# Two attention blocks on one core: load order of the start, one pool for two PSUM banks, and some exponentials on VectorE

## The chip, the cores and the metric

The kernel runs on one core of one Trainium2 chip. The metric is the time of one execution on the device in microseconds (us), lower is better. Times are medians of a few executions. A profile belongs to one execution. I compare each kernel with runs of the kernel before that were taken on the same chip in the same rounds. Executions of one kernel spread by 0.1% to 0.7% here (up to 8 us), so I do not read differences of 2 or 3 us between kernels.

## The reference

Two blocks of 32 heads with head size 32, sequence 2048, model size 1024, everything in bf16; the outputs are concatenated.

```python
# block A: plain multi-head attention over 2048 keys
q, k, v = split_heads(x @ wqkv)                    # 32 heads of 32
p = softmax(q @ k.T * 32 ** -0.5)                  # 2048 x 2048 for every head
a = merge_heads(p @ v) @ wo
# block B: four segments of 512; causal softmax inside a segment,
# plus a linear memory of the earlier segments, mixed by a gate g
for s in range(4):
    a_dot = softmax(q_s @ k_s.T * scale + mask) @ v_s
    a_mem = (phi(q_s) @ M) / (phi(q_s) @ z + 1e-6)
    o_s   = g * a_mem + (1 - g) * a_dot
    M, z  = M + phi(k_s).T @ v_s, z + sum(phi(k_s))
b = merge_heads(o) @ wo
out = concat([a, b], axis=-1)
```

Block A exponentiates 32 x 2048 x 2048 scores, block B some more. That is what the kernel's time goes into.

## The kernel before

The kernel does not write its instructions in a fixed order. While it is being built, it runs a small scheduler: processes ask for engine time, PSUM banks and buffers, and a model of the engines (durations, priorities, pools) decides which instruction comes next on each engine. The result is a fixed order per engine, with semaphores. Any edit, also one of a priority, reorders thousands of instructions. And a process that waits for a bank or buffer from a pool makes the order itself wait.

The kernel uses eight banks of PSUM. Three pairs take scores, one bank (OB) takes the output of the P times V matmuls ("PV"), one bank (SB) takes everything else ("side jobs": projections, memory, output projections).

```python
PAIRS = [(0, 1), (2, 3), (4, 5)]
OB, SB = 6, 7
RING = 20                          # half pairs of exponentiated scores kept in SBUF: 10 pairs

def s_batch(self, u, k):           # one batch of scores: two pairs, 8 matmuls of 256 columns
    ...
    prs = yield acq(self.pairs, npair)            # 2 of the 3 pairs
    ...
    yield do("PE", lambda e: f(e, mms), r=keys, w=w, cost=N256, prio=0, mode=ROW)
    for x in range(npair):
        Q.spawn(self.exps(u, k, x, prs[x], slots[x], one))

def exps(self, u, k, x, pr, sl, one):             # one pair: 128 x 1024 scores
    ...
    yield do("ACT", lambda e: e.activation(ap, self.ps[:, pr[0]:pr[1] + 1, :], ACTF.Exp, scale=SCALE), ...)
    Q.give(self.pairs, [pr])
    ...

def pv_unit(self, u, steps, half):
    ...
    yield acq(self.obank, 1)       # the one output bank; finish() gives it back
    ...

# start (cut): weights first, x behind them, transposing loads of the rest of x at once
for k in (0, 1, 2):
    Q.spawn(self.load_WA(k, 0, 0, "SP" if k == 0 else "ACT"))
Q.spawn(self.rest_x())
```

A batch of scores needs two of three pairs. While ScalarE works on the second pair of a batch, one pair is free, and the other pair that the next batch needs is the one whose exponential (the first of the batch) has just ended. So the scores of the next batch start when the exponential of the first pair has ended, and run while ScalarE works on the second pair.

## Time and profile before

1183.4 us, median of three runs (1181.3 to 1183.8); the profiled one took 1181.5 us on the core. First the page: span, busy times, granted TensorE clock in tenths per fortieth of the span, the chain that ended last, and the costliest group.

```profile
span 1181.5 us, 49521 instructions
...
PE 1061.9 (90%) x23146; PEld 508.2 (43%) x23146; DVE 484.6 (41%) x1070; ACT 1120.2 (95%) x1223; POOL 125.9 (11%) x285
...
PEclk7999998999799999999999999899999999899999
...
ACT 66%; PE 25%; DVE 5%; DMA 2%; issue 1%; POOL 0%; ACTq 0%; SPq 0%; DVEq 0%
...
L861 ACT ACTIVATE PT<-ps 128x1024 bf16<-128x1024 f32 x1168 | 1083.2, 1098 | 24.3 <-PE ps L844 23.6
```

ScalarE (ACT) is the limit and TensorE (PE) is close behind it. The 1168 exponentials of the last line, with 16 more that write other buffers, are nearly the whole of ACT. One record lasts 1098 ns, but that is not what one exponential costs: records overlap. In the trace, neighbouring exponentials start 904 ns apart (median), and I use this distance as the cost. The third row below is what remains of the span, so the ledger sums to it:

| part of the span | before, us |
|---|---|
| until the first exponential starts | 24.2 |
| ScalarE work: 1184 x 0.904 + 32 activations of the memory part | 1094.0 |
| exponentials that start later than that distance ("late") | 45.7 |
| from the end of the last exponential to the end | 17.6 |

The start, in the timeline (start and duration in us; a bracket tells how long the engine was idle and what ended that):

```profile
2.07 1.93 ACTq L549 DMA_DIRECT2D OTA<-in_A_x_dram  x2
...
13.02 2.74 PE L536 MATMUL ps<-ident,OTA 128*128 128x128 bf16 x24 [6.46 <-DMA OTA<-in_A_x_dram]
...
16.91 6.07 PE L591 MATMUL ps<-xA,WA 128*32 128x512 bf16 x64 [1.15 <-issue]
...
24.23 7.44 ACT L861 ACTIVATE WoB<-ps 128x1024 bf16<-128x1024 f32 x8 [7.42 <-PE ps L844]
```

TensorE waits until 13 us for three of the four x tiles, which are queued behind the weights. Then the first 64 projection matmuls take 6.07 us, because the clock is at half from 8.2 to 21.9 us (first digit of the clock row).

### The profile page before, as it was taken

To read this page: it belongs to the slowest core of one execution; us is meant where nothing else is said; L and a number is where in the kernel's file an instruction comes from. 1 tells how busy PE (TensorE), PEld (TensorE's weight loads), DVE (VectorE), ACT (ScalarE), POOL (GpSimd) and SP (SyncE) were. 2 spreads that over 40 slices of the span, in tenths; PEclk is the share of its full clock that TensorE was granted. 3 is DMA by queue.
4 is the path that set the end of the run, shared out by engine and by line. 5 is a ranking of instruction groups with operands and counts; after the bars stand their busy time and mean duration, and the time that the engine had idled before them with its cause. 6 is when DMAs were issued, how large, how long until landed. Compare 5 with 4: busy or idle time off the path is not lost.

```text
span 1181.5 us, 49521 instructions
## 1 busy us (share of the span) xinstructions
PE 1061.9 (90%) x23146; PEld 508.2 (43%) x23146; DVE 484.6 (41%) x1070; ACT 1120.2 (95%) x1223; POOL 125.9 (11%) x285
## 2 busy tenths in 40 slices
PE   6889998988799898999899999889999999899997
PEld 2444443443344444444444444434444444344443
DVE  1224333333343545445434544445355543444232
ACT  2999999999899999999999999999999899999994
POOL 1002002001111111102101201111111110110000
PEclk7999998999799999999999999899999999899999
DMA  9532333224021223251222123131222122101111
GB/s 169 98 59 43 67 95 72 44 56 87 20 60 29 62 45 56 50 89 42 59 48 60 34 56 65 34 69 47 48 55 56 43 47 91 38 25 34 38 39 45
DMA packets 214837, 67.23 MB, mean 57 GB/s; under 512 B 203872, under 2 KB 212064, under 8 KB 214624
## 3 DMA queue, kind: packets, MB, share of 16 engines
q1 hardware_dynamic: 212256, 62.94, 24.8%
q8 instruction: 183, 3.00, 1.1%
q10 hardware_dynamic: 2368, 1.05, 0.4%
q14 instruction: 30, 0.25, 0.1%
HBM read 36.70 MB, written 8.39 MB: 38 GB/s over the span
## 4 chain that ended last, share of the span: by engine, by line
ACT 66%; PE 25%; DVE 5%; DMA 2%; issue 1%; POOL 0%; ACTq 0%; SPq 0%; DVEq 0%
ACT PT L861 64%; PE ps L591 8%; PE ps L937 7%; PE ps L844 4%; PE ps L1003 4%; ACT E L696 2%; DMA OTA<-in_A_x_dram 1%; DVE VT L597 1%; DMA VB<-VT 1%; DMA VA<-VT 1%; ACT WoB L861 1%; DVE Dt L959 1%; DVE md L722 1%; DVE Rb L962 1%; DVE QA L597 0%
## 5 line engine op out<-in xcount | busy, mean ns | idle before, releaser
L861 ACT ACTIVATE PT<-ps 128x1024 bf16<-128x1024 f32 x1168 | 1083.2, 1098 | 24.3 <-PE ps L844 23.6
L937 PE MATMUL ps<-PT,ones 128*32 128x256 bf16 (+1 forms) x4800 | 302.6, 274 | 0.0
L937 PE MATMUL ps<-PT,VA 128*32 128x256 bf16 x4032 | 258.9, 278 | 13.4 <-ACT PT L861 7.4
L844 PE MATMUL ps<-QA,KA 32*128 32x256 bf16 x4096 | 206.6, 276 | 33.1 <-ACT PT L861 26.5
L591 PE MATMUL ps<-xA,WA 128*32 128x512 bf16 x3072 | 218.2, 389 | 10.3 <-DVE md L722 2.2
L591 PE MATMUL ps<-xB,WB 128*32 128x512 bf16 x3072 | 213.8, 381 | 14.5 <-DVE QA L597 3.7
L870 POOL TENSOR_SCALAR_AFFINE_SELECT PT<-PT 128x256 bf16<-128x256 bf16 (+1 forms) x224 | 98.5, 440 | 900.2 <-ACT PT L861 893.9
L937 PEld LDWEIGHTS ps<-PT,VA 128*32 128x32 bf16 x4032 | 107.7, 96 | 104.7 <-issue 42.3
L844 PEld LDWEIGHTS ps<-QA,KA 32*128 32x128 bf16 x4096 | 61.1, 92 | 205.7 <-ACT PT L861 182.9
L937 PEld LDWEIGHTS ps<-PT,ones 128*32 128x32 bf16 x4800 | 130.3, 98 | 21.7 <-issue 0.5
L591 PEld LDWEIGHTS ps<-xA,WA 128*32 128x32 bf16 x3072 | 73.0, 97 | 83.7 <-issue 27.0
L591 PEld LDWEIGHTS ps<-xB,WB 128*32 128x32 bf16 x3072 | 74.3, 96 | 79.5 <-issue 45.4
L959 DVE STREAM_TRANSPOSE Dt<-ps 128x256 f32<-128x256 f32 x128 | 57.2, 447 | 124.2 <-PE ps L937 123.3
L597 DVE CAST KQB<-ps 128x512 bf16<-128x512 f32 x64 | 44.0, 688 | 147.5 <-PE ps L591 147.5
L1009 DVE CAST outsb<-ps 128x512 bf16<-128x512 f32 x61 | 42.0, 689 | 118.8 <-PE ps L1003 118.8
L597 DVE CAST VT<-ps 128x512 bf16<-128x512 f32 x64 | 43.8, 684 | 95.0 <-PE ps L591 92.2
L1003 PE MATMUL ps<-WoB,OTB 128*32 128x512 bf16 x1024 | 71.4, 381 | 2.0 <-DVE outsb L1009 0.7
L1003 PE MATMUL ps<-xA,OTA 128*32 128x512 bf16 x1024 | 67.2, 384 | 1.0 <-DVE outsb L1009 0.7
L937 PE MATMUL ps<-PT,VB 128*32 128x256 bf16 (+1 forms) x768 | 47.6, 269 | 13.5 <-DVE tB L984 3.8
L962 DVE STREAM_TRANSPOSE Rb<-Rall 128x256 f32<-128x256 f32 x128 | 56.6, 442 | 3.6
L597 DVE CAST KA<-ps 128x512 bf16<-128x512 f32 x32 | 22.0, 689 | 67.3 <-PE ps L591 67.3
L844 PE MATMUL ps<-KQB 32*128 32x128 bf16 (+3 forms) x512 | 43.7, 304 | 3.8 <-ACT PT L861 2.2
(70 smaller groups left out, 466.5 us busy)
## 6 DMA issues: line engine op xcount, KB each, us to landing
WB<-in_B_wk_dram SPq DMA_DIRECT2D x32, 256.0 KB, 2.9
WB<-in_B_wq_dram SPq DMA_DIRECT2D x32, 256.0 KB, 2.9
WB<-in_B_wv_dram SPq DMA_DIRECT2D x32, 256.0 KB, 3.2
out_dram<-outsb SPq DMA_DIRECT2D x64, 128.0 KB, 1.8
WA<-in_A_wqkv_dram SPq DMA_DIRECT2D x22, 256.0 KB, 2.9
WoB<-in_B_wo_dram SPq DMA_DIRECT2D x1, 2048.0 KB, 9.7
xA<-in_A_wo_dram SPq DMA_DIRECT2D x1, 2048.0 KB, 8.5
WA<-in_A_wqkv_dram ACTq DMA_DIRECT2D x2, 256.0 KB, 5.8
```

Of the source, the lines that this page charges most:

```text
L591: ins = e.matmul(self.ps[32 * c:32 * c + 32, bank, :], W[:, i, 32 * c:32 * c + 32], x(i), start=(i == 0), stop=(i == NI - 1))
L597: return e.tensor_copy(dst, self.ps[:, bank, :])
L696: yield do("ACT", lambda e: e.activation(self.E[:, k0:k1, :], KQ[:, k0:k1, :], ACTF.Exp), r=kq, w=["E"], cost=0.093 + 0.427 * nk, prio=-1)
L722: yield do("DVE", lambda e: e.transpose(self.md[:, :], self.ps[:, bank, :]), r=[("ps", bank)], w=["md"], cost=dve(512), prio=1)
L844: ins = e.matmul(self.ps[:, bk, col:col + w], lhs(t, hs), rhs(q0, w, hs), start=True, stop=True)
L861: yield do("ACT", lambda e: e.activation(ap, self.ps[:, pr[0]:pr[1] + 1, :], ACTF.Exp, scale=SCALE), r=[("ps", bk) for bk in pr], w=keys, ...
L870: yield do("POOL", lambda e, m=m, n=n: e.affine_select(m, m, pattern=[[0, n], [1, P]], compare_op=ALU.is_ge, fill=0.0, base=0, channel_mul ...
L937: ins = e.matmul(out, l, r, start=st, stop=sp)
L959: yield do("DVE", lambda e: e.transpose(Dt[:, :], den), r=[("ps", OB)], w=[("Dt", x)], cost=dve(QU), prio=0)
L962: yield do("DVE", lambda e: e.transpose(Rb[:, :].rearrange("p (a b) -> p a b", b=32), self.spread(Rc)), r=[("Rc", ui)], w=[("Rb", x)], cos ...
L1003: ins = e.matmul(self.ps[32 * c:32 * c + 32, bank, :], lhs(j)[:, 32 * c:32 * c + 32], W(j), start=(j == 0), stop=(j == NG - 1))
L1009: return f(self.outsb[ob][:, :], self.ps[:, bank, :])
```

## The change

Its intent: let ScalarE start earlier, take a little work off it, and keep the score matmuls on time. The diff has some 260 changed lines; cut to its core:

```diff
 # start: x first, then the weights; the transposing loads wait until x has landed
-        for k in (0, 1, 2):
-            Q.spawn(self.load_WA(k, 0, 0, "SP" if k == 0 else "ACT"))
+        def first_w():
+            yield ("ev", ("XS", 2)); yield ("ev", ("XS", 3))
+            Q.spawn(self.load_WA(0, 0, 0, "SP")); Q.spawn(self.load_WA(1, 0, 0, "ACT"))
+            ...
 # start: warm-up matmuls behind each of the four groups of transposes
+            yield self.warm((4, 4, 4, 8)[t])
 # output bank and side bank in one pool, PV first
-            yield acq(self.obank, 1)
+        OB, = yield acq(self.side, 1, -1000)
 # 43 times: one bank of the second pair of a batch is exponentiated on VectorE
+        if (u, k, x) in self.off:                  # x is always 1
+            Q.spawn(self.exps_dve(pr[1], ...))     # six VectorE operations
+            yield do("ACT", lambda e: e.activation(..., self.ps[:, pr[0], :], ACTF.Exp, scale=sc), ...)
 # exps_dve: 2^t from bits. The exponent is kept as it is, the fraction goes through a cubic
+        z = max(scores, -122 * 2**23) + BIAS       # to int32, reads PSUM
+        u = (z & 0x7fffff) | 0x3f800000            # fraction, as a float in 1..2
+        z = z & 0x7f800000                         # power of two
+        p = (((u + C2) * u + C1) * u + C0) * z     # three scalar_tensor_tensor
 # memory for it: ring 20 -> 26 half pairs, one output buffer of block B instead of two
-RING = 20
+RING = 26
-        self.OTB = [sb(f"OTB{i}", [P, NG, 512]) for i in range(2)]
+        self.OTB = sb("OTB", [P, NG, 512])
 # the scheduler's model: margins for waits, a longer tail of PE; its parameters chosen anew
-    par = dict(b=(18, 14, 10), mem=-2, memM=2, span=66, rate=0.58, ahead=20, sl=4, ...)
+    par = dict(b=(14, 10, 3), mem=-4, memM=2, span=50, rate=0.6, ahead=20, sl=5, ..., mg=0.05, off=0.75, ...)
```

Also: the queries of block A are scaled in their projection so that `exps_dve` can read the exponent from the bits of a score, block B's operation T is merged into the next one, output buffers go from six to four, projections hold their place on TensorE once begun, PV goes first at the end, and the last drain of the output overlaps the reading of a flag.

## The prediction

> **What bounds the kernel now.** ScalarE. The page gives ACT 1120 us of a 1181.5 us span (95%), and the chain of waits is 66% ACT, nearly all of it the 1184 exps of a 128x1024 bank pair. In the timeline neighbouring exps start 904 ns apart (median), so they take 1184 x 0.904 = 1070 us; the 32 exps of E add 24 us. The first exp starts at 24.2 us, the last ends at 1163.6 us: 1139 us for 1094 us of work, so 45 us go to late starts (the view of waits names 31 us: score matmuls not there). The rest is a 24 us start and an 18 us tail. PE is 90% busy, DVE 41%.
>
> **What the change does, costed.**
> 1. Start. Weights are queued first now, and the last x tiles land only at about 13 us; the clock is at half from 8.2 to 21.9 us, so the 64 first projection matmuls take 6.1 us. With x first, transposing loads held back and warm-up matmuls in between, I expect x at 7 us, projection from 10 us, mostly at full clock (3.5 us), first exp at 15 us: 9 us saved, all on the path.
> 2. VectorE exps. 0.75 x 58 units = 43 half pairs go to DVE. ACT work falls by 512 elements each, 904 to an estimated 477 ns, 18 us in all. Not all arrives: a batch needs two of three pairs, so its scores start only after the exp of the previous batch's first half ends (its start + 1.05 us), plus the median 0.18 us until PE starts, 0.40 us of score matmuls, 0.05 us. That loop of 1.6 to 1.7 us fits in 2 x 0.904 but not in 0.904 + 0.477. I count 0.15 to 0.2 us each: 7 us. DVE pays six operations, about 3.7 us each time, 160 us in all: DVE goes to some 55%.
> 3. One pool for output and side banks, a ring of 13 instead of 10 pairs, margins in the order, PE's latency modelled longer. The next output can start while the last is normalised, but side jobs then lack a bank. I give it 13 of the 45 us of late exps. No engine work is saved, except the T operation (11 us of DVE, off the path).
> 4. Tail. PV goes first once scores are done (now 30 groups of projection matmuls come first, 6.6 us), and the output drain overlaps the flag read: 4 us.
>
> Sum: 1183 - 9 - 7 - 13 - 4 = 1150; I say 1149 us, 80% in 1132 to 1165. Chances: faster 0.80, same 0.18, slower 0.02.
>
> **What would show it.** First exp at 13 to 18 us. 43 ACT activations of 128x512 from PSUM, ACT busy near 1100. Behind each of them a gap on ACT of 0.15 to 0.35 us, waiting for scores; if those gaps are missing, step 2 is worth 18 us. DVE busy 610 to 660 us. Late exps below 35 us apart from those gaps. Last exp to end 13 to 15 us.
>
> **What would make it wrong.** PE becomes the limit: its work is unchanged while the span shrinks, so it would be 93% busy, and the window 900 to 950 us (PE 48 of 50 us, ACT 46.4) is already bound by it. Half-clock episodes (41 us after the start) fall differently with every order. Longer DVE queues delay evacuations and so side banks. If the new order removes most late exps, the time is below 1135.
>
> The Trainium skill ("ScalarE: Activation LUTs", Rules for kernel authors) has ScalarE as the only option for exp; the change bypasses that with bit operations and a cubic.

## The result, and the profile after

1155.0 us, median of four runs (1154.4 to 1159.7), against 1183.6 us for the kernel before in the same rounds (1181.3 to 1187.1). The ratio is 0.9765, 95% interval 0.9729 to 0.98. The same lines of the page:

```profile
span 1153.8 us, 49786 instructions
...
PE 1050.9 (91%) x23164; PEld 507.3 (44%) x23165; DVE 626.9 (54%) x1302; ACT 1103.9 (96%) x1223; POOL 127.4 (11%) x285
...
PEclk9999999999999999999999999999999999989999
...
ACT 55%; PE 32%; DVE 7%; DMA 4%; issue 1%; SPq 0%; POOL 0%; DVEq 0%
...
L891 ACT ACTIVATE PT<-ps 128x1024 bf16<-128x1024 f32 x1125 | 1045.3, 1101 | 21.3 <-PE ps L864 19.2
```

ScalarE is busy for 16 us less, VectorE for 142 us more, and TensorE and VectorE stand on the chain more often. The start, in the timeline:

```profile
9.11 0.61 PE L552 MATMUL ps<-ident,OTA 128*128 128x128 bf16 x8
...
11.38 3.64 PE L612 MATMUL ps<-xA,WA 128*32 128x512 bf16 x64
...
16.27 7.44 ACT L891 ACTIVATE WoB<-ps 128x1024 bf16<-128x1024 f32 x8 [5.49 <-PE ps L864]
```

The projections start 5.5 us earlier and run at full clock, 3.64 us instead of 6.07. The ledger, for the one profiled execution of each kernel:

| part of the span, us | before | after | difference |
|---|---|---|---|
| first exponential starts | 24.2 | 16.3 | -8.0 |
| ScalarE work | 1094.0 | 1075.6 | -18.4 |
| late, directly behind a half exponential | 0 | 15.4 | +15.4 |
| late, all others | 45.7 | 30.6 | -15.1 |
| tail | 17.6 | 15.8 | -1.8 |
| span | 1181.5 | 1153.8 | -27.7 |

(Differences are of the unrounded values.) The second and third row belong together. The 43 half exponentials take 43 x (0.904 - 0.477) = 18.4 us off ScalarE, and ScalarE then stands still for 15.4 us right behind them. One of them, in the timeline of the kernel after (lines of other work are left out):

```profile
107.33 2.08 ACT L891 ACTIVATE PT<-ps 128x1024 bf16<-128x1024 f32 x2
...
108.10 0.69 DVE L916 TENSOR_SCALAR ze<-ps 128x512 int32<-128x512 f32 x1 [0.73 <-PE ps L864]
...
109.14 0.77 ACT L885 ACTIVATE PT<-ps 128x512 bf16<-128x512 f32 x1
...
109.50 0.12 PEld L864 LDWEIGHTS ps<-QA,KA 32*128 32x128 bf16 x8 [0.42 <-ACT PT L891]
109.50 0.40 PE L864 MATMUL ps<-QA,KA 32*128 32x256 bf16 x8
...
109.95 2.85 ACT L891 ACTIVATE PT<-ps 128x1024 bf16<-128x1024 f32 x3
```

The two exponentials of the first line end at 109.41; the second of them is the first pair of the batch. The scores of the next batch follow at 109.50, 0.09 us later, and the exponential of these scores at 109.95. The half one (L885) started at 109.14 and could have let the next go at 109.62, so 0.33 us are lost. VectorE was not what held this up: its read of the other half (L916) was over by 108.79, and in all 43 cases it was over before the exponential ahead of the half one ended. In the 43 cases the scores start 0.056 us (median; up to 0.5 us where TensorE was busy with other work) after the exponential before the half one ended, and the next exponential starts 0.449 us (median) after the scores did; 0.346 us (median) of the 0.427 us saved are lost.

What the 43 pieces cost on VectorE, grouped by line (count, then busy time in us and mean ns of one):

```profile
L924 DVE SCALAR_TENSOR_TENSOR PT<-we,ze 128x512 bf16<-128x512 f32 x43 | 29.5, 686 | 0.8
L922 DVE SCALAR_TENSOR_TENSOR we<-ue 128x512 f32<-128x512 f32 x43 | 29.5, 686 | 0.0
L923 DVE SCALAR_TENSOR_TENSOR we<-we,ue 128x512 f32<-128x512 f32 x43 | 29.4, 685 | 0.6
L916 DVE TENSOR_SCALAR ze<-ps 128x512 int32<-128x512 f32 x43 | 28.9, 672 | 16.7 <-PE ps L864 16.7
L921 DVE TENSOR_SCALAR ze<-ze 128x512 int32<-128x512 int32 x43 | 18.1, 420 | 0.6
L919 DVE TENSOR_SCALAR ue<-ze 128x512 int32<-128x512 int32 x43 | 18.0, 417 | 0.3
```

These sum to 153 us, 3.57 us for each half bank that saves ScalarE 0.43 us. The two masks are the cheap ones, at 420 ns against 686 for the three `scalar_tensor_tensor`. That resembles what the Trainium skill states ("VectorE: DVE Perf Modes", the perf-mode tier table): it has fp32 `tensor_scalar` in SBUF in the 2x mode and fp32 `tensor_tensor` in the 1x mode; neither int32 nor `scalar_tensor_tensor` is in the table; here the int32 masks were the faster ones, like the former, and the `scalar_tensor_tensor` the slower ones, like the latter.

### The profile page after: what moved, and what is told of

Same layout as the page of the kernel before. It is cut to its first block, busy times and chain, and to the rows that moved or that the text cites. A ratio compares the mean times of both kernels' runs of the same rounds, so it can differ in the third digit from the quotient of the medians.

```text
span 1153.8 us, 49786 instructions
## 1 busy us (share of the span) xinstructions
PE 1050.9 (91%) x23164; PEld 507.3 (44%) x23165; DVE 626.9 (54%) x1302; ACT 1103.9 (96%) x1223; POOL 127.4 (11%) x285
## 4 chain that ended last, share of the span: by engine, by line
ACT 55%; PE 32%; DVE 7%; DMA 4%; issue 1%; SPq 0%; POOL 0%; DVEq 0%
ACT PT L891 52%; PE ps L612 12%; PE ps L994 9%; PE ps L864 6%; PE ps L1062 4%; DMA xB<-in_B_x_dram 2%; ACT E L718 1%; DVE Rb L1021 1%; DVE Dt L1018 1%; DMA VA<-VT 1%; DVE ze L916 1%; DVE VT L618 1%; DMA PKt<-PH 1%; ACT PT L885 1%; POOL PT L900 0%
## 5 line engine op out<-in xcount | busy, mean ns | idle before, releaser
L891 ACT ACTIVATE PT<-ps 128x1024 bf16<-128x1024 f32 x1125 | 1045.3, 1101 | 21.3 <-PE ps L864 19.2
L994 PE MATMUL ps<-PT,ones 128*32 128x256 bf16 (+1 forms) x4800 | 296.3, 274 | 0.0
L994 PE MATMUL ps<-PT,VA 128*32 128x256 bf16 x4032 | 252.6, 278 | 17.1 <-ACT PT L891 7.7
L864 PE MATMUL ps<-QA,KA 32*128 32x256 bf16 x4096 | 206.3, 276 | 47.7 <-ACT PT L891 42.6
L612 PE MATMUL ps<-xB,WB 128*32 128x512 bf16 x3072 | 208.1, 387 | 12.0 <-DMA xB<-in_B_x_dram 3.5
L612 PE MATMUL ps<-xA,WA 128*32 128x512 bf16 x3072 | 200.5, 381 | 2.1 <-DVE VT L618 0.5
L864 PEld LDWEIGHTS ps<-QA,KA 32*128 32x128 bf16 x4096 | 61.0, 92 | 214.6 <-ACT PT L891 192.8
L994 PEld LDWEIGHTS ps<-PT,VA 128*32 128x32 bf16 x4032 | 107.9, 97 | 84.1 <-issue 25.9
L994 PEld LDWEIGHTS ps<-PT,ones 128*32 128x32 bf16 x4800 | 129.9, 98 | 24.5 <-issue 0.3
L1018 DVE STREAM_TRANSPOSE Dt<-ps 128x256 f32<-128x256 f32 x128 | 56.4, 441 | 24.2 <-PE ps L994 23.3
L1062 PE MATMUL ps<-WoB,OTB 128*32 128x512 bf16 x1024 | 67.1, 381 | 0.5 <-DVE md L742 0.2
L1062 PE MATMUL ps<-xA,OTA 128*32 128x512 bf16 x1024 | 65.0, 381 | 0.3 <-DVE outsb L1068 0.2
L994 PE MATMUL ps<-PT,VB 128*32 128x256 bf16 (+1 forms) x768 | 46.2, 267 | 8.2 <-DVE OTA L1025 3.2
L864 PE MATMUL ps<-KQB 32*128 32x128 bf16 (+3 forms) x512 | 43.4, 302 | 3.9 <-ACT PT L891 2.9
L619 DVE TENSOR_SCALAR QA<-ps 128x512 bf16<-128x512 f32 x32 | 22.0, 688 | 41.0 <-PE ps L612 41.0
```

Source lines behind the costliest of these rows:

```text
L612: ins = e.matmul(self.ps[32 * c:32 * c + 32, bank, :], W[:, i, 32 * c:32 * c + 32], x(i), start=(i == 0), stop=(i == NI - 1))
L619: return e.tensor_scalar(dst, self.ps[:, bank, :], scale, None, ALU.mult)
L864: ins = e.matmul(self.ps[:, bk, col:col + w], lhs(t, hs), rhs(q0, w, hs), start=True, stop=True)
L994: ins = e.matmul(out, l, r, start=st, stop=sp)
L1018: yield do("DVE", lambda e: e.transpose(Dt[:, :], den), r=[("ps", OB)], w=[("Dt", x)], cost=dve(QU), prio=0, hold=0.15)
L1062: ins = e.matmul(self.ps[32 * c:32 * c + 32, bank, :], lhs(j)[:, 32 * c:32 * c + 32], W(j), start=(j == 0), stop=(j == NG - 1))
```

## The experiments

Theory after reading the result: the gain is 8 us of the start, 15 us of other late exponentials (which I had put down mainly to the shared pool), 2 us of tail, and almost nothing from VectorE's exponentials. Rivals: the halves help indirectly, through TensorE catching up in the gaps; the 15 us come from the ring, from the scheduler's margins, or from nothing but a fortunate order.

The kernel after serves as base unless I say otherwise. Twelve kernels ran, all gave correct results. "Late" is as in the ledger, "others" are the late ones not directly behind a half. Where I write "parameters chosen anew", I built several hundred settings of the scheduler's parameters for that variant and took the one whose planned order was shortest in the kernel's own planning; every time below is from the chip. All ratios are to the kernel before.

| kernel | median us | ratio [95%] | first exp | behind halves | others late | tail |
|---|---|---|---|---|---|---|
| after | 1155.0 | 0.9765 [0.9729, 0.9800] | 16.3 | 15.4 | 30.6 | 15.8 |
| no_dve_exps | 1155.5 | 0.9753 [0.9723, 0.9784] | 15.9 | 0 | 30.0 | 14.4 |
| no_dve_exps_tuned | 1159.8 | 0.9791 [0.9763, 0.9819] | 16.1 | 0 | 33.7 | 14.6 |
| half_first | 1167.4 | 0.9873 [0.9833, 0.9913] | 15.9 | 0.2 | 55.1 | 17.5 |
| old_start_loads | 1163.5 | 0.9819 [0.9788, 0.9850] | 24.5 | 15.5 | 32.0 | 15.6 |
| no_warm | 1156.0 | 0.9764 [0.9735, 0.9794] | 13.6 | 14.8 | 28.1 | 15.9 |
| own_obank | 1176.9 | 0.9935 [0.9895, 0.9974] | 16.9 | 14.7 | 52.6 | 15.3 |
| own_obank_tuned | 1157.8 | 0.9760 [0.9723, 0.9798] | 18.0 | 14.8 | 33.7 | 15.4 |
| ring20_tuned | 1162.2 | 0.9797 [0.9764, 0.9831] | 16.1 | 15.5 | 37.4 | 15.0 |
| neighbour | 1179.6 | 0.9945 [0.9910, 0.9980] | 15.9 | 13.6 | 55.9 | 17.6 |
| neighbour_b | 1170.6 | 0.9892 [0.9861, 0.9924] | 16.0 | 13.2 | 48.6 | 15.6 |
| hf_obank_tuned | 1147.7 | 0.9695 [0.9662, 0.9729] | 17.0 | 0.2 | 36.1 | 15.5 |
| hf_obank_b | 1146.0 | 0.9677 [0.9654, 0.9700] | 17.1 | 0.2 | 32.3 | 15.8 |

This table leaves out the granted clock, which differs between the kernels. In the profiled executions, between the first and the last exponential, some stretches run at half clock, and many of the other late exponentials start in these stretches or up to 1 us behind them (my count, good to a few us):

| kernel | half clock, us | others late there | others late elsewhere |
|---|---|---|---|
| before | 41 | 11 | 34 |
| after | 34 | 10 | 20 |
| no_dve_exps | 24 | 6 | 24 |
| own_obank | 72 | 27 | 26 |
| own_obank_tuned | 65 | 16 | 17 |
| hf_obank_tuned | 37 | 14 | 22 |
| hf_obank_b | 24 | 8 | 24 |

### No exponentials on VectorE: no_dve_exps and no_dve_exps_tuned

```diff
-    par = dict(..., off=0.75, ...)
+    par = dict(..., off=0.0, ...)
```

> The kernel after, with no half exp on VectorE (1184 full exps on ScalarE again), the rest unchanged. My theory: a half exp in the second pair of a batch gives back 0.35 of its 0.43 us, as the next scores wait for the exp of the first pair, so this part is worth 43 x 0.08 = 3 us and this kernel is at about 1158 us (1154 to 1162). Rival: the wait behind the halves lets PE catch up, so that part of the other late exps is spared too, and the part is worth its 18 us of ScalarE work: about 1173 us. A second rival is that VectorE's extra 160 us delay evacuations, so that this kernel is even faster than the kernel after.

Measured: 1155.5 us. The whole part is worth nothing that these runs can show; the first rival (18 us) falls clearly. In the ledger the 18.4 us of ScalarE work come back, the 15.4 us behind the halves go away, and the others stay, 30.0 against 30.6. So in sum no more than a few us of other waits were spared by the waits behind the halves or caused by VectorE's extra 153 us (second rival). A few us either way stay open: no_dve_exps was granted a little more clock (0.988 to 0.990 in its four executions, against 0.980 to 0.986), and away from half clock its others are 24 us against 20. My 3 us are within the spread.

> No half exps on VectorE, scheduling parameters chosen anew. If the exps on VectorE in the second pair are worth nothing, this is at or a little under 1155 us (1151 to 1156). If they are worth several us under a fitting order, then choosing anew does not help here and it stays at 1155 or above, as that order was already good.

Measured: 1159.8 us with parameters chosen anew for it, so choosing anew did not help. By the letter of what I had written, this leaves room for a gain of a few us from the VectorE exponentials. Since the same kernel with the old parameters took 1155.5 us, I take no more from it than that two orders of one kernel differ by 4 us, and that the better planned one was not the faster one.

### The half exponential in the first pair: half_first

If a half in the second pair is lost because the next scores wait for the first pair, then a half in the first pair should not be: it ends earlier, so the scores start earlier, and a full exponential hides them.

```diff
-                        self.off.add((u, k, 1))
+                        self.off.add((u, k, 0))
```

(and the same index where PV puts this batch later)

> The kernel after, with the 43 half exps moved from the second to the first pair of their batch. My theory: then the scores of the next batch wait for the half exp (done 0.43 us earlier) and a full exp of 0.90 us hides them, so the gap on ScalarE behind a half exp falls from a median of 0.35 us to under 0.1 us, and the time falls by 8 to 15 us, to about 1143 us. Rival: the pair is held by VectorE's first operation (0.69 us) or PE is the limit; then the gaps only move and the time stays within 4 us of 1155.

Measured: 1167.4 us, slower by 12 us, so the time missed my range altogether. But the gaps behind the halves did what the theory says; they are gone, 0.2 us for all 43. In the timeline:

```profile
107.32 0.69 DVE L916 TENSOR_SCALAR ze<-ps 128x512 int32<-128x512 f32 x1 [0.73 <-PE ps L864]
...
107.45 0.76 ACT L885 ACTIVATE PT<-ps 128x512 bf16<-128x512 f32 x1
107.93 5.78 ACT L891 ACTIVATE PT<-ps 128x1024 bf16<-128x1024 f32 x6
...
108.29 0.40 PE L864 MATMUL ps<-QA,KA 32*128 32x256 bf16 x8
```

The half starts at 107.45, the next full one 0.48 us later without a wait. The time was lost elsewhere: the others rose by 24.5 us, half of that in one place. ScalarE's own timeline, then TensorE's, around it:

```profile
590.68 1.94 ACT L891 ACTIVATE PT<-ps 128x1024 bf16<-128x1024 f32 x2 [0.20 <-PE ps L864]
605.29 1.94 ACT L891 ACTIVATE PT<-ps 128x1024 bf16<-128x1024 f32 x2 [12.67 <-PE ps L864]
```

```profile
592.57 0.23 PE L994 MATMUL ps<-PT,ones 128*32 128x128 bf16 x4
593.33 1.91 PE L1062 MATMUL ps<-WoB,OTB 128*32 128x512 bf16 x32 [0.53 <-DVE VT L618]
...
604.52 0.28 PE L994 MATMUL ps<-PT,VB 128*32 128x256 bf16 x4
...
604.84 0.40 PE L864 MATMUL ps<-QA,KA 32*128 32x256 bf16 x8
```

From 592.8 to 604.5 us TensorE runs only projections and memory matmuls: no PV (L994) and no scores (L864). It is not short of work, the scores are just not in the order there. PV and scores stop and resume together, while the output rows of a segment of block B are projected (L1062) from the buffer OTB, of which the change had left one out of two. By the code, an output of block B now takes one of two small buffers (tB) before its PV begins and keeps it until the memory part is ready and the previous segment's rows have been projected; without PV no place in the ring comes free, and without a place no scores are issued. I did not test this chain by a run of its own, so it is argued, not shown.

### Is it the order? Two controls: neighbour and neighbour_b

The last run raised a doubt about all of them: perhaps any edit costs some 10 or 20 us, as the parameters had been chosen for exactly the kernel after. So I moved one parameter by one step, and another one, without any change of engine work.

```diff
-    par = dict(..., sl=5, ...)
+    par = dict(..., sl=4, ...)          # neighbour
```
```diff
-    par = dict(..., span=50, ...)
+    par = dict(..., span=56, ...)       # neighbour_b
```

> A control: the kernel after with one scheduling parameter moved by one step (sl 5 to 4: from how few free ring pairs on the outputs get priority). No engine work changes. My theory now: the order of the kernel after is a lucky one of many, so that such a step alone costs 5 to 20 us (about 1165 us), as much as the parts that I undid singly. Rival: the order is robust, the time stays within 3 us of 1155, and the 21 us of the run with its own output bank is the value of the shared pool.

> A second control: the kernel after with the parameter span moved from 50 to 56 (how far ahead of use the projections are ordered). No engine work changes. If the order of the kernel after is one lucky order among many, this is slower too, by 5 to 25 us, most of it in one or two long waits for scores near 600 or 850 us. If only the other parameter (sl) was special, it is within 4 us of 1155.

Measured: 1179.6 us and 1170.6 us, that is 25 and 16 us slower than the kernel after, out of a gain of 29 us. The view of waits, ScalarE for score matmuls (sum in us, times, longest), of the kernels before and after, half_first, neighbour and neighbour_b, in this order:

```profile
ACT PT L861 <- PE ps L844: 23.6, 36, 1.6
```
```profile
ACT PT L891 <- PE ps L864: 19.2, 30, 1.6
```
```profile
ACT PT L891 <- PE ps L864: 32.6, 28, 12.7
```
```profile
ACT PT L891 <- PE ps L864: 40.1, 35, 9.8
```
```profile
ACT PT L891 <- PE ps L864: 34.9, 35, 9.8
```

The last number is what to look at. The bad orders hold single waits of 10 to 13 us; they end at 605 us (half_first), 857 us (neighbour) and 607 us (neighbour_b). In neighbour two more, of 6.7 us (before 613 us) and 4.0 us (before 69 us), make up 21 of its 25 us together with the first. (This view counts only idle time after a record's end, so its sums are smaller than the ledger's.) The kernel after has no long wait. A run that undoes a part and is slower therefore proves nothing about the part unless the parameters are chosen anew for it, and even then one order stands for each kernel.

### The shared pool: own_obank and own_obank_tuned

```diff
-        OB, = yield acq(self.side, 1, -1000)
+        OB, = yield acq(self.obank, 1)
-        self.side = Pool([SB, OB])
+        self.side = Pool([SB]); self.obank = Pool([OB])
```

(and the three places that give the bank back)

> The kernel after, with the output bank and the side bank fixed as in the kernel before, the rest unchanged. My theory: most of the 15 us of late exps that went away (other than behind half exps) came from the shared pool, so that late exps rise by 8 to 15 us and the time is about 1166 us. Rival: the gain came from the deeper ring and the margins of the order; then the time is within 4 us of 1155.

> The output bank fixed again as in own_obank, but with scheduling parameters chosen anew for it (ahead, b, mg, od, span). If the shared pool is worth something by itself, this stays at 1165 us or above; if the 21 us were only a bad order under parameters chosen for another kernel, it comes to 1150 to 1158 us, with late exps near those of the kernel after.

Measured: 1176.9 us with the parameters of the kernel after, as if the pool were worth 22 us, more than I had expected of it. Its longest wait for scores is 3.7 us; half of its late time falls into 72 us of half clock, so it is not bad in the way of the three above. With parameters chosen anew (ahead 22, b (16, 12, 6), mg 0.045, od 10, span 48) it took 1157.8 us, and its other late exponentials are 33.7 us against 30.6. So in these two orders the pool is worth some 3 us, which is within the spread, and own_obank_tuned had less clock on top (0.970 to 0.978 against 0.980 to 0.986). My theory, that most of the 15 us came from the pool, falls.

### The ring: ring20_tuned

```diff
-RING = 26
+RING = 20
```

(with parameters chosen anew; they put 36 halves on VectorE instead of 43)

> The kernel after with the ring of score buffers back at 10 pairs instead of 13, scheduling parameters chosen anew with it. If the deeper ring is what the late exps owe their fall to, late exps (other than behind half exps) are over 40 us and the time is 1163 us or more; if it is not, choosing anew brings it to 1153 to 1160 us, like the run with its own output bank.

Measured: 1162.2 us, other late exponentials 37.4 us. That lies between my two cases: 7 us more than in the kernel after, where orders of one kernel differ by as much. The deeper ring may be worth some us; the run does not settle it.

### The start: old_start_loads and no_warm

```diff
-        Q.spawn(first_w())                                   # old_start_loads
+        for k in (0, 1, 2):
+            Q.spawn(self.load_WA(k, 0, 0, "SP" if k == 0 else "ACT"))
-        yield ("ev", ("WA", 1, 0))                           # rest_x: when the transposing loads go
+        yield ("ev", ("XS", 3))
-                         r=[("XS", 3), ("XS", 2), ...] if c == 1 and t == 0 else [], w=...
+                         w=...
```
```diff
-            yield self.warm((4, 4, 4, 8)[t])                 # no_warm
+            pass
```

> The kernel after, with only the load order of the start put back: weights first, transposing loads not held back for the x tiles. Warm-up matmuls stay. My theory: the order of the loads is worth most of the 8 us by which the first exp starts earlier: first exp at 21 to 24 us, time about 1160 to 1163 us. Rival: the warm clock made the gain; then the first exp starts at 17 to 19 us and the time is under 1158 us.

> The kernel after without the warm-up matmuls between the transposes of the start (the first eight stay). I read the first exp, not the total. If the clock matters, the first 64 projection matmuls take about 6 us instead of 3.6 and the first exp starts at 17 to 19 us; if only the order of the loads matters, it starts at or before 16 us, and the matmuls were only in the way of the transposes.

Measured, old_start_loads: first exponential at 24.5 us, time 1163.5 us, other parts of the ledger as in the kernel after. The load order is the whole gain of the start; the run put back both sides of it together (weights first, transposing loads not held), so it does not part them. From its timeline:

```profile
17.38 0.61 PE L552 MATMUL ps<-ident,OTA 128*128 128x128 bf16 x8
...
19.65 3.64 PE L612 MATMUL ps<-xA,WA 128*32 128x512 bf16 x64
...
24.54 1.94 ACT L891 ACTIVATE WoB<-ps 128x1024 bf16<-128x1024 f32 x2 [5.50 <-PE ps L864]
```

With the late x tiles the warm-up matmuls did keep the clock for the projections (3.64 us), but they also stood in the way, so that the first exponential came no earlier than in the kernel before. From the timeline of no_warm:

```profile
4.64 2.92 PE L552 MATMUL ps<-ident,OTA 128*128 128x128 bf16 x32
...
8.71 3.64 PE L612 MATMUL ps<-xA,WA 128*32 128x512 bf16 x64 [1.15 <-ACT xA L561]
...
13.59 1.94 ACT L891 ACTIVATE WoB<-ps 128x1024 bf16<-128x1024 f32 x2 [4.98 <-PE ps L864]
```

Without the warm-up matmuls between the transposes the clock is full all the same (granted from 6.7 us on in this trace, from 5.5 us in the kernel after), and the first exponential starts at 13.6 us, 2.7 us earlier than in the kernel after. So in this profiled execution they only cost time. The total does not show it (1156.0 us; the profiled execution was the fastest, 1150.0, the others took up to 1157.6).

### Both together: hf_obank_tuned and hf_obank_b

half_first showed that the saved ScalarE time is real, and own_obank_tuned that the pool is not needed. So: halves in the first pair, output bank fixed, parameters chosen anew (two sets).

```diff
-                        self.off.add((u, k, 1))
+                        self.off.add((u, k, 0))
-        OB, = yield acq(self.side, 1, -1000)
+        OB, = yield acq(self.obank, 1)
-    par = dict(b=(14, 10, 3), ..., span=50, rate=0.6, ahead=20, ..., pv=18, ob=2, ..., od=8, ...)
+    par = dict(b=(15, 10, 4), ..., span=58, rate=0.585, ahead=22, ..., pv=19, ob=3, ..., od=2, ...)   # hf_obank_b
```

> Half exps in the first pair of their batch (the 43 us x 0.43 = 18 us of ScalarE work really saved), output bank fixed, scheduling parameters chosen anew. My theory: gaps behind half exps under 0.05 us, other late exps near 30 us, so about 1155 - 15 = 1140 us (1136 to 1146). Rival: PE is the limit (91% busy) and the saved ScalarE time comes back as other late exps, as in half_first (42 us apart from one 13 us wait); then about 1153 us.

> Half exps in the first pair and the output bank fixed, with a second set of scheduling parameters (near the first). If the 1148 us of the first set comes from the ScalarE work really saved, this is at 1144 to 1152 us as well; if it was a lucky order alone, it is at 1155 or above.

Measured: 1147.7 us, just outside my range of 1136 to 1146, and 1146.0 us with the second set (from a longer search), inside the range that I gave for that one. Both beat the kernel after (ratios 0.9695 and 0.9677 against 0.9765). The gaps behind halves are 0.2 us, the others 36.1 and 32.3. The nearest comparison is own_obank_tuned, which has the same bank layout, halves in the second pair, and parameters from a search as long as that of hf_obank_tuned: 1157.8 us. By the medians, 10 to 12 us of the 14.6 us that the gaps behind its halves cost arrived in the time (8 to 10 by the ratios).

This comparison has a flaw: own_obank_tuned was granted less clock (0.970 to 0.978, against 0.978 to 0.989 for the two), and its executions take longer with less of it (1159.7 us at 0.970, 1152.6 at 0.978). At the same 0.978 hf_obank_tuned took 1149.2 and 1151.0 us, so part of the 10 to 12 us may be the clock. The kernels without halves do not have this flaw: no_dve_exps and no_dve_exps_tuned had 0.983 to 0.990, no less on the whole than the two, and took 1155.5 and 1159.8 us. Against them the halves in the first pair gain 8 to 14 us of the 18.4, though the bank layout differs as well. That the gaps are gone is shown; how much of them arrives in the time is known only this roughly.

The view of waits of hf_obank_b, ScalarE for score matmuls:

```profile
ACT PT L891 <- PE ps L864: 12.4, 20, 1.3
```

There is no long wait in it. I did not run it without the warm-up matmuls of the start.

## Why the prediction was right or wrong

The measured 1155.0 us lies in the predicted range, 6 us above the 1149 us. Part of that closeness is luck: the halves and the tail brought less than predicted, and the largest term, the late exponentials, came out without its cause being known. The terms of the sum:

- **Start, 9 us predicted, 8.0 measured.** Right in mechanism. The load order did it, which old_start_loads shows (back to 24.5 us). I had counted the warm-up matmuls as part of the gain; no_warm shows that they cost 2.7 us here.
- **VectorE exponentials, 7 us predicted, 3.0 in the ledger, nothing in the time.** The step that failed is the size: "I count 0.15 to 0.2 us each". The mechanism that I had derived (scores wait for the exponential of the first pair, so that a half behind it comes too soon) is what the trace shows, and the predicted gaps of 0.15 to 0.35 us are there, with a median of 0.346 us, at the edge. My loop of 1.6 to 1.7 us leaves 0.11 to 0.2 us of each half, of which I took the upper part; its own terms sum to 1.68 us. In the trace, the exponential behind a half starts 1.73 us (0.904 + 0.823, medians) after the one before the half, where 1.38 us are offered. The main miss is the exponential of the first pair: I took it as over 1.05 us after its start, and these records last 1.18 us (median). Each half brings 0.08 us instead of 0.15 to 0.2 us, 3 us in all, and that is too little to be seen in the time.
- **Late exponentials, 13 us predicted, 15.1 measured.** Right in size; that is luck as far as the runs show, since the cause is open. I had named the pool, the ring and the margins together, the pool first. own_obank_tuned does without the pool at 33.7 us of late ones against 30.6. The two neighbours show that the choice of parameters alone moves this number between 30.6 and 55.9 us. How much of the 15 us belongs to the deeper ring, to the margins in the scheduler's model or to the choice of parameters remains open; no run took the margins away.
- **Tail, 4 us predicted, 1.8 measured.** Too high, and 15.8 us is outside the 13 to 15 us that I gave; the tail of other kernels with this code is 14.4 to 17.6 us, so its share is not clear of the order either.
- **What I warned of.** TensorE at 93% would have been the new limit: it came to 91%, and the halves moved to the first pair still gained several us, so it was not a hard limit. Between the first and the last exponential, half clock lasted 41 us before and 34 us after, and the others late in it were 11 and 10 us: of the 15 us, about 1 us.
- VectorE's busy time was predicted at 610 to 660 us and is 626.9; ACT near 1100 and is 1103.9.

## What to carry to other kernels

Before work is moved off the limiting engine, follow what the next piece on that engine waits for: here 43 half exponentials saved 18.4 us of work, and 15.4 us came back as waits, because the producer of the next scores was released by the piece before, not by the shortened one; shortening the other piece of each pair left only 0.2 us of such waits, and once the order was chosen anew the time fell (by 8 to 14 us against the kernels without halves). In a kernel whose order comes from a tuned scheduler, take a control first that changes a parameter and no work: here such a step cost 16 to 25 us, so an ablation says something only after its parameters have been chosen anew. Compare the granted clocks too before reading what is left. When a start is slow, first ask which load is needed first, and only then whether the clock is warm.

## What the Trainium skill lacked or had wrong

- "ScalarE: Activation LUTs", Rules for kernel authors: says that ScalarE is the only option for exp. Here VectorE computed it in six operations, at 3.57 us for 128x512 against 0.43 us saved on ScalarE. The page could give this price.
- The same page, What ACT_TABLE_LOAD costs: an ACTIVATE with immediates takes 186 ns + 0.833 ns per element, and neighbours overlap by about 93 ns, which makes 946 ns (estimate from the page) between starts at 1024 elements and 520 ns at 512. That is right for the 32 activations of the kernel before that read SBUF: the next one starts 947 and 520 ns (medians) after them. It is 43 ns too much for the exponentials, which read PSUM: 904 ns, and 476 to 481 ns at 512 elements in half_first. The section does not tell the two sources apart (another page of the skill does). A record's length (1098 ns in the mean) is no cost.
- "TensorE: Matmul & The Clock Gate", Part 4: PE-mode transpose: says that the full clock does not engage for transpose mode, as it does not count as busy in the same way. In no_warm TensorE ran transposes from 4.64 to 7.56 us and nothing else; the full clock was granted at 6.7 us, in the middle of them, and lasted through a further 1.15 us of idleness (the matmuls behind took 3.64 us for 64, full rate). Plain matmuls had run until then from 1.24 us, so no run shows whether transposes alone would raise the clock, but they did not prevent it. In the kernel before, 2.74 us of transposes from 13.02 us ran at half clock and full clock came only at 21.9 us, 5 us into the projections, which would fit the page.
